# Order of two VectorE subtractions in the outputs' products of a hash-attention and feed-forward kernel

## The chip, the cores and the metric

The kernel runs on one core of a Trainium2 chip. The metric is the device time of one execution in microseconds, as a median over several runs. The engines of the core work side by side, each through its own queue: TensorE (PE in the profile) multiplies matrices, VectorE (DVE) and GpSimd (POOL) do elementwise work, ScalarE (ACT) does activations and copies, SyncE (SP) issues most of the transfers. [...]

## The reference

Attention in which a query sees the keys of its own hash bucket, and behind it a feed-forward block with a quick GELU. All numbers are 32-bit floats.

```
def _attn_setup():
    batch, n_heads, seq, head_dim = (4, 8, 768, 64)
...
    mask = q_bucket[:, :, :, None] == k_bucket[:, :, None, :]
    scores = scale * np.matmul(q, k.transpose(0, 1, 3, 2))
    scores = np.where(mask, scores, -1000000000.0)
...
    return np.matmul(attn, v).astype(np.float32)
...
def _moe_ref(x, w_in, w_out) -> np.ndarray:
    h = x @ w_in
    g = h * (1.0 / (1.0 + np.exp(-1.702 * h)))
    return (g @ w_out).astype(np.float32)
...
    x = np.ascontiguousarray(attn_out.transpose(0, 2, 1, 3)).reshape(B * S, H * D)
```

x is 3072 x 512, w_in 512 x 2048, g 3072 x 2048, w_out 2048 x 512. This case is about the last product, g @ w_out.

## The kernel before

The kernel has three stages: attention (to about 316 us of the span), the hidden layer x @ w_in with its GELU (to 594 us), and the outputs g @ w_out (from 594 us on). The order of the instructions of TensorE, VectorE, ScalarE and GpSimd is the order in which the program writes them; only SyncE's transfers are placed by the scheduler.

**Two levels of seven products.** The outputs are made in Strassen's manner (Winograd's variant, on two levels): instead of eight products of quarter matrices there are seven, of sums of the quarters. On the outer level the tokens come in 3 blocks of 1024, and each block takes the seven outer products in the order `OUTER` (L707). That makes 21 steps (`steps_out`, L1022). The outer sums of g were made and written to `g_dram` in the stage before. Each step is again done with seven inner products, `product_of_halves` (L1063).

**One step.** `fetch` (L1025) brings one outer operand of g (2 MB, in two halves of 1 MB) into one of two places that take turns: `raw_g` for even steps and a part of `s_in` for odd ones. Its four quarters are b11 and b12 (first half), b21 and b22 (second half); a quarter is 128 partitions x 4 x 256. Four subtractions, `sums_b` (L219 to L225), make the right operands of the inner products from them:

- t1 = b12 - b11 (L222)
- d12 = b22 - b12, written over b12 (L223)
- t2 = b22 - t1 (L224)
- t4 = b21 - t2 (L225)

t1, t2 and t4 have rooms of their own: t1a and t2a for even steps, t1b and t2b for odd ones (in step 1 a part of `t_x`), and one t4g. The left operands, quarters of w_out and their sums, are in SBUF; GpSimd makes the sums for later steps (`inner_sums`, L1232, behind a `mark`, L1231).

The products take their right operands in this order: product 1 b11, 2 b21, 3 b22, 6 t2, 7 d12, 5 t1, 4 t4 (`RIGHT`, L706, gives the place of each in the list b11, d12, b21, b22, t1, t2, t4; in the last step product 2 comes after product 5). A product is eight matmuls of 128x128 by 128x256 (L1074), each behind its own weight load. It goes to one of eight PSUM banks in turn. ScalarE copies products 1 and 3 out (L1087, L1090); VectorE adds the others up (L1078).

**Where the sums stand in VectorE's queue.** The sums of step n + 1 are issued during step n. `product_of_halves` calls `after(0)` to `after(3)` at four places between its additions, and `after` (L1237) picks from the list that `g_sums(n + 1)` (L1044) gives:

```
steps = [later_sums[at : at + 1]] if n == 0 else [[], later_sums[0:1], later_sums[1:3], later_sums[3:], []][at : at + 1]
```

So in a usual step the first of the list follows the additions of products 6 and 7, the second and third follow those of product 5, and the fourth follows that of product 4. In step 0 they go one to each place. In the last step but one `after(2)` gives the second and third in the same way, and the fourth stands between transposes. The sums of step 0 itself are issued at the end of the last two tiles of the hidden layer (L1216): `g_sums(0)[:1]` and `g_sums(0)[1:]`.

VectorE's queue also holds the outer additions (L1267, L1268) and the transposes of finished outputs into y (`turned`, L1049), which `written` (L1056) sends out.

Of the kernel before, what the change touches and what calls it, by code (L numbers as in the profile page):

```python
# [38 lines left out]
def kernel(  # L39
# [17 lines left out]
    nc = tc.nc  # L57
# [161 lines left out]
    def sums_b(eng, b11, b12, b21, b22, t1, t2, t4):  # L219


        return [lambda: eng.tensor_tensor(t1, b12, b11, op=Alu.subtract),  # L222
                lambda: eng.tensor_tensor(b12, b22, b12, op=Alu.subtract),  # L223
                lambda: eng.tensor_tensor(t2, b22, t1, op=Alu.subtract),  # L224
                lambda: eng.tensor_tensor(t4, b21, t2, op=Alu.subtract)]  # L225
# [472 lines left out]
    def feed_forward(tag, late=()):  # L698
# [9 lines left out]
        with ExitStack() as fctx:  # L708
# [313 lines left out]
            steps_out = [(sb, o) for sb in range(n1) for o in OUTER]  # L1022
# [10 lines left out]
            def g_quarters(n):  # L1033
                if n not in g_tiles:


                    g_tiles[n] = wholes[4:6] if n == 1 else [
                        (st2 if n % 2 else gp).tile([P, F4, TH], F32, tag=t, name=t + "ab"[n % 2]) for t in ("t1", "t2")]
                    g_tiles[n] = g_tiles[n] + [gp.tile([P, F4, TH], F32, tag="t4", name="t4g")]
                g = raw_g[n % 2]  # L1040
                x = [g[:, F4 * k : F4 * (k + 1), TH * j : TH * (j + 1)] for k in range(2) for j in range(2)]
                return x + g_tiles[n]

            def g_sums(n):  # L1044
                return sums_b(nc.vector, *g_quarters(n)) if n < len(steps_out) else [lambda: None] * 4

            ys = {}

# [152 lines left out]
            for n in range(2 * NESTED.stop, 3 * MT):  # L1201
                sb, mt = divmod(n, MT)
                if n == 2 * NESTED.stop + 1:
                    assert not agenda
                    inner_ctx.close()
                    twice_ctx.close()
                    cv_ctx.close()
                    sets[:] = [fctx.enter_context(tc.tile_pool(name=f"f{2 + i}{tag}", bufs=1, space=PSUM, side=side))
                               for i, side in enumerate(("right", "left"))]
                    gp = fctx.enter_context(tc.tile_pool(name=f"gp{tag}", bufs=1))  # L1210
                    raw_g[0] = gp.tile([P, FC // 2, XT], F32, name="raw_g")
                    t_ctx = fctx.enter_context(ExitStack())
                    places_of_sums.append(t_ctx.enter_context(tc.tile_pool(name=f"ts{tag}", bufs=1)))
                    outer_sums(*heads.pop("sums"))
                    fetch(0)
                t = {3 * MT - 2: g_sums(0)[:1], 3 * MT - 1: g_sums(0)[1:]}.get(n, []) if n > 3 * MT - 3 else []  # L1216
                hidden(sb, mt, between.get(n, []) + ([lambda: fetch(1)] if n == 3 * MT - 1 else []), t + todo.pop(n, []))
                yield
# [6 lines left out]
            for n, (sb, o) in enumerate(steps_out):  # L1225
# [6 lines left out]
                for f in {2: inner_sums(3), 3: inner_sums(4), 5: inner_sums(5) + inner_sums(6)[:2], 6: inner_sums(6)[2:]}.get(n, []):  # L1232
                    f()
                later_sums = g_sums(n + 1)
                m = wholes[n % len(wholes)]

# [91 lines left out]
```

## Time and profile before

| what | us |
|---|---|
| median of 3 runs (lowest, highest) | 859.61 (859.51, 860.23) |
| the profiled execution, its own time | 859.85 |
| its span | 858.0 |
| outputs' stage, 594 to 858: first product to last | 594.07 to 849.66 |
| one inner product, from start to start of the next | 1.73 |
| one subtraction of 128x1024 on VectorE, alone | 1.22 |
| the same beside GpSimd's sums (t2 of step 0, d12 of step 1) | 2.29, 2.28 |
| one addition of 128x256 on VectorE, alone | 0.42 |

Share of the engines in some stretches of the outputs' stage, each about one step (busy us; the last row is the tail):

| stretch, us | length | PE | DVE | POOL |
|---|---|---|---|---|
| 594.0 to 606.2 (step 0) | 12.20 | 12.20 | 11.79 | 10.34 |
| 606.2 to 618.3 (step 1) | 12.10 | 12.10 | 11.11 | 9.92 |
| 618.3 to 631.2 (step 2) | 12.90 | 12.26 | 12.52 | 5.73 |
| 631.2 to 644.0 (step 3) | 12.80 | 12.30 | 11.43 | 0.60 |
| 644.0 to 656.1 (step 4) | 12.10 | 12.10 | 8.32 | 7.14 |
| 837.4 to 858.0 (last step and tail) | 20.60 | 12.26 | 12.58 | 0.00 |

Times in the profile are microseconds from the span's start. A line of the order of time gives start, length, engine, line of the kernel, operation, out<-in, shape and count; in square brackets stands how long the engine was idle before it and what ended that, which is inferred from the events of the semaphores. PEld is TensorE's weight load. The ends of matmuls are modelled, so a product's cost is best read from the starts of two products.

### The profile page before, as it was taken

The numbers are of one execution on the slowest core, as the hardware profiler recorded it, in microseconds if no ns is written. First come the engines' busy times: TensorE is split into PE (matmuls) and PEld (weight loads), VectorE is DVE, ScalarE is ACT, GpSimd is POOL, SyncE is SP. The second block draws the span as 40 slices with busy tenths as digits, with TensorE's granted clock in tenths as the row PEclk, the third lists the DMA queues.
The fourth block names the chain that finished last, engine by engine and source line by source line (L and its number), as shares of the span: only waits on it lengthen the run. The fifth ranks groups of instructions, "written<-read, shape, count | busy, mean of one in ns | idle before, by whom it ended". The sixth has DMA issues, their size and how long they took to land.

```text
span 858.0 us, 13647 instructions
## 1 busy us (share of the span) xinstructions
PE 846.6 (99%) x5007; PEld 529.2 (62%) x5007; DVE 703.7 (82%) x1072; ACT 344.9 (40%) x549; POOL 353.4 (41%) x316
## 2 busy tenths in 40 slices
PE   9999999999999999999999999999999999999996
PEld 4444444444444444566666665545888888888885
DVE  4589999999999885788988788577998977797776
ACT  5866667777666644343443444433000000000000
POOL 4343333433333359996854476669724000000000
PEclk9999999999999999999999999999999999999998
DMA  5636655445653104435555646587744675467524
GB/s 130 98 52 107 105 94 85 85 86 100 116 91 75 47 26 152 142 143 226 199 201 213 221 162 231 196 292 252 264 165 166 198 258 194 155 191 245 196 99 101
DMA packets 160987, 132.11 MB, mean 154 GB/s; under 512 B 122608, under 2 KB 137616, under 8 KB 155536
## 3 DMA queue, kind: packets, MB, share of 16 engines
q1 hardware_dynamic: 152016, 106.63, 44.6%
q10 hardware_dynamic: 8896, 24.53, 8.3%
q8 instruction: 41, 0.67, 0.3%
q14 instruction: 34, 0.28, 0.1%
HBM read 79.69 MB, written 50.33 MB: 152 GB/s over the span
## 4 chain that ended last, share of the span: by engine, by line
PE 95%; DVE 3%; DMA 1%; issue 0%; ACT 0%; ACTq 0%; SPq 0%; DVEq 0%
PE product L1074 27%; PE product L751 22%; PE ps L435 18%; PE av L468 15%; PE small L819 6%; PE product L819 3%; PE dn L489 1%; DVE xT L1078 1%; PE hash L411 1%; DMA q<-in_q_dram 1%; DVE y L1054 1%; DVE v L1078 0%; PE hash L376 0%; DVE t2a L224 0%; DVE raw_g L223 0%
## 5 line engine op out<-in xcount | busy, mean ns | idle before, releaser
L436 ACT ACTIVATE e<-ps 128x768 f32<-128x768 f32 x192 | 151.2, 812 | 25.7 <-PE ps L435 23.1
L435 PE MATMUL ps<-qT,kT 64*128 64x384 f32 x768 | 155.1, 482 | 0.0
L443 POOL TENSOR_TENSOR acc<-e 128x768 f32<-128x768 f32 x32 | 51.8, 1618 | 194.0 <-ACT e L436 174.5
L468 PE MATMUL av<-e,v 128*32 128x385 f32 x1536 | 128.0, 487 | 0.0
L751 PE MATMUL product<-xT,w_in_sb 128*128 128x512 f32 x216 | 100.1, 593 | 0.1
L468 PEld LDWEIGHTS av<-e,v 128*32 128x32 f32 x1536 | 48.5, 109 | 76.2 <-issue 74.5
L435 PEld LDWEIGHTS ps<-qT,kT 64*128 64x128 f32 x768 | 68.0, 187 | 38.5 <-issue 38.4
L751 PE MATMUL product<-t_x,s_in 128*128 128x512 f32 x192 | 89.4, 592 | 0.0
L1087 ACT COPY u<-product 128x256 f32<-128x256 f32 x21 | 7.8, 372 | 173.4 <-PE product L1074 140.2
L751 PEld LDWEIGHTS product<-xT,w_in_sb 128*128 128x128 f32 x216 | 40.9, 190 | 36.5 <-issue 32.9
L435 PE MATMUL ps<-qf,kf 64*128 64x384 bf16 x384 | 62.9, 324 | 0.1
L444 POOL TENSOR_TENSOR acc<-acc,e 128x768 f32<-128x768 f32 x32 | 55.8, 1744 | 2.5
L751 PEld LDWEIGHTS product<-t_x,s_in 128*128 128x128 f32 x192 | 36.5, 190 | 29.7 <-issue 26.8
L449 DVE SCALAR_TENSOR_TENSOR acc<-e 128x768 f32<-128x768 f32 x32 | 47.7, 1490 | 5.1 <-ACT e L436 5.1
L767 DVE TENSOR_TENSOR u<-product,u 128x256 f32<-128x256 f32 (+1 forms) x60 | 28.4, 486 | 16.3 <-PE product L819 13.1
L435 PEld LDWEIGHTS <-kf 64*128 64x128 bf16 x384 | 18.9, 94 | 35.1 <-issue 6.2
L451 DVE TENSOR_TENSOR acc<-acc,e 128x768 f32<-128x768 f32 x32 | 34.3, 1072 | 3.3
L451 DVE TENSOR_TENSOR acc<-acc,acc 128x768 f32<-128x768 f32 x32 | 31.2, 974 | 6.3 <-POOL acc L444 3.2
L1074 PE MATMUL product<-raw_g,xT 128*128 128x256 f32 x152 | 35.1, 379 | 0.0
L222 POOL TENSOR_TENSOR u<-v,u 128x1024 f32<-128x1024 f32 (+1 forms) x11 | 23.8, 2165 | 22.1 <-ACT v L764 8.1
L767 DVE TENSOR_TENSOR v<-product,v 128x512 f32<-128x512 f32 x24 | 16.5, 689 | 19.4 <-PE product L751 19.4
L767 DVE TENSOR_TENSOR c<-small,c 128x256 f32<-128x256 f32 (+1 forms) x54 | 24.2, 461 | 8.8 <-PE small L819 8.6
(278 smaller groups left out, 1727.4 us busy)
## 6 DMA issues: line engine op xcount, KB each, us to landing
raw_g<-g_dram SPq DMA_DIRECT2D x22, 1024.0 KB
s_in<-g_dram SPq DMA_DIRECT2D x20, 1024.0 KB
g_dram<-c ACTq DMA_DIRECT2D x18, 512.0 KB
raw<-in_moe_w_out_dram ACTq DMA_DIRECT2D x16, 512.0 KB
raw<-in_moe_w_in_dram SPq DMA_DIRECT2D x15, 512.0 KB
v<-in_v_dram SPq DMA_DIRECT2D x32, 192.0 KB
k<-in_k_dram SPq DMA_DIRECT2D x60, 96.0 KB
q<-in_q_dram SPq DMA_DIRECT2D x60, 96.0 KB
```

The costliest lines, as they stand in the source:

```text
L222: return [lambda: eng.tensor_tensor(t1, b12, b11, op=Alu.subtract), lambda: eng.tensor_tensor(b12, b22, b12, op=Alu.subtract), lambda: eng ...
L435: nc.tensor.matmul(ps[:, j, 0:HS], a[hs, keys], m[hs, cols], start=not last, stop=last)
L436: nc.scalar.activation(es[c][:, kt, :, 0:HS], ps[:, :, 0:HS], Act.Exp, scale=1.0 / D**0.5)
L443: nc.gpsimd.tensor_tensor(acc, es[c][:, 0, :, 0:HS], es[c][:, 1, :, 0:HS], op=Alu.add)
L444: nc.gpsimd.tensor_tensor(acc, acc, es[c][:, 2, :, 0:HS], op=Alu.add)
L449: nc.vector.scalar_tensor_tensor(acc, e[0], T * TINY, e[1], op0=Alu.add, op1=Alu.add)
L451: nc.vector.tensor_tensor(acc, acc, x, op=Alu.add)
L468: nc.tensor.matmul(av[D * j + d : D * j + d + 32, :], vt[:, t, j, d : d + 32], es[c][:, t, j, :], start=(t == 0), stop=(t == T - 1))
L751: nc.tensor.matmul(ps, wq[LEFT[i]][:, kc, :], xq[RIGHT[i]][:, kc, :], start=(start and kc == 0), stop=(kc == K2 - 1), skip_group_check=not ...
L767: nc.vector.tensor_tensor(dst, x, y, op=Alu.add)
L819: nc.tensor.matmul(x, wq[LEFT[i]], xq[RIGHT[i]], start=start, stop=True, skip_group_check=True)
L1074: nc.tensor.matmul(ps, wq[LEFT[i]][:, c, :], gq[RIGHT[i]][:, c, :], start=(c == 0), stop=(c == F4 - 1))
```

## The change

`g_sums` gives the same four subtractions in another order: t1, t2, d12, t4. Since `after` and L1216 pick by position, t2 is issued where d12 was and d12 where t2 was, in all 21 steps. The other users of `sums_b` keep their order.

```
             def g_sums(n):
-                return sums_b(nc.vector, *g_quarters(n)) if n < len(steps_out) else [lambda: None] * 4
+                if n == len(steps_out):
+                    return [lambda: None] * 4
+                t1, d12, t2, t4 = sums_b(nc.vector, *g_quarters(n))
+                return [t1, t2, d12, t4]
```

In a usual step both stand next to each other in VectorE's queue. In step 0, which issues the sums of step 1, the additions of product 5 stand between them.

## The prediction

> **What bounds the kernel now.** I read the page's busy times and chain first, then TensorE's waits, then the order of time of three engines around the two waits found there. Steps are counted 0 to 20 as the kernel runs them (21 tiles of the outputs), and a step's seven products run in the order 1, 2, 3, 6, 7, 5, 4 (in the last 1, 3, 6, 7, 5, 2, 4).
>
> ```profile
> PE 846.6 (99%) x5007; PEld 529.2 (62%) x5007; DVE 703.7 (82%) x1072; ACT 344.9 (40%) x549; POOL 353.4 (41%) x316
> PE 95%; DVE 3%; DMA 1%; issue 0%; ACT 0%; ACTq 0%; SPq 0%; DVEq 0%
> ```
>
> TensorE is busy for 99% of the span and is 95% of the chain that ended last. So only time in which TensorE stands still can be won, and the outputs' stage has two such places (columns: total us, times, longest us; window from 560 us to the end):
>
> ```profile
> PE product L1074 <- DVE t2a L224: 0.6, 1, 0.6
> PE product L1074 <- ACT xT L1090: 0.5, 1, 0.5
> ```
>
> Matmuls in order of time (start, length, operands), products 3, 6, 7 of step 2 and then of step 3:
>
> ```profile
> 621.70 1.89 PE L1074 MATMUL product<-raw_g,w_in_sb 128*128 128x256 f32 x8
> 624.23 1.96 PE L1074 MATMUL product<-t2a,w_in_sb 128*128 128x256 f32 x8 [0.64 <-DVE t2a L224]
> 626.03 1.89 PE L1074 MATMUL product<-raw_g,xT 128*128 128x256 f32 x8
> ...
> 634.66 1.89 PE L1074 MATMUL product<-s_in,w_in_sb 128*128 128x256 f32 x8
> 637.05 1.96 PE L1074 MATMUL product<-t2b,w_in_sb 128*128 128x256 f32 x8 [0.49 <-ACT xT L1090]
> 638.85 1.89 PE L1074 MATMUL product<-s_in,w_out_sb 128*128 128x256 f32 x8
> ```
>
> Undisturbed, two products start 3.45 us apart (618.25 to 621.70), one 1.73. Here two take 626.03 - 621.70 = 4.33 and 638.85 - 634.66 = 4.19. The two places lose 0.88 and 0.74, together **1.62 us**; the waits' own 0.64 and 0.49 are less because a restarted product also runs 0.07 slower and matmul ends are modelled. No other product of the 21 steps starts late. Weight loads, where the wait sits:
>
> ```profile
> 621.49 1.70 PEld L1074 LDWEIGHTS product<-raw_g,w_in_sb 128*128 128x128 f32 x8
> 624.20 1.59 PEld L1074 LDWEIGHTS product<-t2a,w_in_sb 128*128 128x128 f32 x8 [1.01 <-ACT xT L1090]
> ...
> 634.45 1.70 PEld L1074 LDWEIGHTS product<-s_in,w_in_sb 128*128 128x128 f32 x8
> 637.01 1.59 PEld L1074 LDWEIGHTS product<-t2b,w_in_sb 128*128 128x128 f32 x8 [0.87 <-ACT xT L1090]
> ```
>
> And VectorE, which makes the operands:
>
> ```profile
> 621.73 1.21 DVE L223 TENSOR_TENSOR raw_g<-raw_g 128x1024 f32<-128x1024 f32 x1
> 622.87 1.21 DVE L224 TENSOR_TENSOR t2a<-raw_g,t1a 128x1024 f32<-128x1024 f32 x1
> ...
> 634.59 1.22 DVE L223 TENSOR_TENSOR s_in<-s_in 128x1024 f32<-128x1024 f32 x1
> 635.72 1.22 DVE L224 TENSOR_TENSOR t2b<-s_in,t1b 128x1024 f32<-128x1024 f32 x1
> ...
> 640.77 0.42 DVE L1078 TENSOR_TENSOR xT<-product,v 128x256 f32<-128x256 f32 x1 [1.24 <-PE product L1074]
> ```
>
> t2 ends at 622.87 + 1.21 = 624.08 and at 636.94; product 6, which reads it, loads its first weights at 624.20 and 637.01, 0.12 and 0.07 later. That the records name ScalarE's copy (c12, L1090) is a coincidence: the copy follows product 3's end by its own 0.4 us and happens to end at 636.96. In step 4 product 6 starts at 649.21, before that copy even starts (649.41). So **t2 is the last thing product 6 waits for, in steps 2 and 3 only**, and d12, made just ahead of it, is not read until product 7, one product later. VectorE is late there because of work before: from 614.99 to 640.77 its only idle time is 0.20 us, so it paces itself.
>
> **The change, part by part.** Nothing is added or removed; two subtractions of 128x1024 change places, in each of the 21 steps. Both wait for the half of g that holds b22 and t1 came before either, so no fetch is needed earlier; t2's room was last read by product 6 two steps before, over 20 us back; no DMA is issued by either. VectorE's total stays: 1.13 us from the start of the one to the start of the next, in either order.
>
> *Step 2.* t2 takes d12's place: 621.73 to 622.94. Product 6's weights are due at 621.49 + 1.73 = 623.22, later than 622.94 + 0.12 = 623.06: the wait is gone, with 0.16 to spare. TensorE is 0.88 ahead. d12 now ends at 624.08; product 7's weights are due at 623.22 + 1.73 = 624.95, so 0.87 is left.
>
> *Step 3.* VectorE has no wait that the 0.88 could shorten, so t2 comes in d12's place at 634.59 to 635.81, released at 635.88. Product 6's weights are due at 634.45 - 0.88 + 1.73 = 635.30: a wait of 0.58 **stays**. They start at 635.88 instead of 637.01, which is **1.13 us** earlier. So the two gains do not add to 1.62: the second place decides, and it moves by the one subtraction that was ahead of t2. d12 ends at 636.94, product 7's weights are due at 635.88 + 1.62 (637.01 to 638.63) = 637.50: 0.56 left. Behind that load TensorE's whole queue would wait.
>
> *From step 4 on.* VectorE's next wait, 1.24 before 640.77, is for product 7 of step 3; with that 1.13 earlier it shrinks to 0.11, and VectorE, its banks, POOL's marked sums and SyncE's refills (released by products and by t4) follow 1.13 earlier. What is late next: in steps 4 to 20 product 6 already finds t2 ready (least slack 0.22, step 6: 672.95 against weights at 673.17; it gains 1.13), and product 7 finds d12 ready with at least that slack plus 1.73, as d12 takes t2's old end. In steps 0 and 1 nothing waits before or after (d12 ends by about 598.3 and 610.8, product 7's weights at 600.76 and 612.85). In the tail (last step) VectorE's line runs through both subtractions whatever their order, after a wait for TensorE, so it moves as a block. If that cover failed, a slow d12 beside POOL (2.28 in step 1 against 1.22) would cost 2.28 - 1.22 - 0.56 = 0.5 in step 3; but POOL has no work from 631.8 to 648.7 there.
>
> *A new wait.* Before, product 7 needed no signal of its own for d12, since t2 came after it. Now it needs one, 21 times. The trace does not show that exact wait. Lower bound 0: product 6 waits for t2 by its own signal in every step, and where it is satisfied (the 19 steps other than 2 and 3) product 7 follows 1.72 to 1.73 later, like any other. Upper bound: the 0.14 from t2's end to the first matmul at a stall that really waits (624.09 to 624.23), times 21 = 2.9. I take 0, the same kind of wait on the same queue.
>
> [...]
>
> *Sum:* 859.85 (the profiled execution: span 858.0 and 1.85 around it) - 1.13 = 858.72; that execution lies 0.24 above the median of 859.61, so the median should be **858.5** (0.13% less).
>
> **Rivals.** A change under 0.2% (1.72 us) is about what a measurement of this kernel can't tell from none.
>
> 1. *Both places close*: 858.0. For it: both waits name nothing else. Against: VectorE has no gap between 626.8 and 636 to make t2 of step 3 earlier. It would need 0.58 us, for instance from the contended 1.24 to 1.94 us adds at 629.4 to 632.5 beside POOL. Even this is within 0.2%.
> 2. *Gain taken back later*: 859.6. A refill of g or a drain that is hidden by less than 1.13 in one of steps 4 to 20 catches TensorE up. Against: in the 200 us from 637 TensorE never waits, and refills are released by TensorE itself. For: their slack is not shown. That the order of the two instructions does not reach the chip gives the same time; VectorE's queue is kept in written order, so hardly possible.
> 3. *The new wait costs* (the slower side): product 7 pays for its own signal in every step. With c per step the time is 858.5 + 21c; from c = 0.054 it is slower at all, from (1.72 + 1.13)/21 = 0.136 slower by over 0.2%. At the bound, 0.14, 861.4. Against: product 6's satisfied waits.
> 4. *More than is lost now*: faster by over 1.72 would need TensorE time outside the two places, for instance VectorE beside POOL in another phase. All that TensorE loses in the steps is 1.62, so this needs the tail (about 8 us after the last matmul) to shrink too.
>
> **How the numbers follow.** Forecast 0.58, rival 1 0.12, rival 2 0.13, rival 3 0.10 (slower by over 0.2% in most of that), rival 4 0.07. Rival 1 and the forecast can pass 1.72 only with the runs' own spread (859.51 to 860.23, 0.7 us); I put 0.10 of their 0.70 there. So: faster 0.17, same 0.74, slower 0.09. The range runs from rival 1 less half that spread, 857.7, to rival 2 with a little of it, 859.8; it leaves out most of rival 3 and rival 4.
>
> **What would show it.** Right: t2 starts near 621.7 and 634.6 in the new trace, TensorE has no wait in step 2 and one of some 0.5 for t2 in step 3, VectorE's wait of 1.24 is nearly gone, the chain of the 200 us after starts 1.1 earlier and the tail is as long as before. Wrong: a wait of product 7 for d12 (L223), products farther apart than 1.73, a new wait for a transfer, or no wait at all in step 3 (rival 1). A time above 859.8 or below 857.7 would make the prediction wrong.

## The result and the profile after

The changed kernel takes 858.70 us (median of 22 runs, 857.98 to 859.58) against 859.75 (22 runs, 859.02 to 861.25): 1.05 us less, a ratio of 0.9987 with a 95% interval of 0.9982 to 0.9993. The interval leaves out 1, so it is faster, by 0.13%. Its profiled execution spans 856.8 us.

From the page of the changed kernel, busy times and the chain's shares by engine:

```profile
PE 846.2 (99%) x5007; PEld 529.2 (62%) x5007; DVE 703.3 (82%) x1072; ACT 344.9 (40%) x549; POOL 353.4 (41%) x316
PE 96%; DVE 2%; DMA 1%; ACT 0%; issue 0%; ACTq 0%; SPq 0%; DVEq 0%
```

The work is the same (703.3 us of VectorE against 703.7), and TensorE still makes up nearly all of the chain. TensorE's waits in the outputs' stage (total us, times, longest):

```profile
PE product L1077 <- issue: 0.2, 1, 0.2
```

Two waits of 0.6 and 0.5 us have become one of 0.2, for which the record names no other engine ("issue"). Products 3, 6 and 7 of step 2, then of step 3, in order of time (a matmul line moved from L1074 to L1077):

```profile
621.45 1.89 PE L1077 MATMUL product<-raw_g,w_in_sb 128*128 128x256 f32 x8
623.17 1.89 PE L1077 MATMUL product<-t2a,w_in_sb 128*128 128x256 f32 x8
624.90 1.89 PE L1077 MATMUL product<-raw_g,xT 128*128 128x256 f32 x8
...
633.53 1.89 PE L1077 MATMUL product<-s_in,w_in_sb 128*128 128x256 f32 x8
635.67 1.97 PE L1077 MATMUL product<-t2b,w_in_sb 128*128 128x256 f32 x8 [0.25 <-issue]
637.47 1.89 PE L1077 MATMUL product<-s_in,w_out_sb 128*128 128x256 f32 x8
```

The weight load of product 6 of step 3:

```profile
635.64 1.59 PEld L1077 LDWEIGHTS product<-t2b,w_in_sb 128*128 128x128 f32 x8 [0.62 <-issue]
```

From product 3 to product 7, step 2 now takes 624.90 - 621.45 = 3.45 us, undisturbed, and step 3 takes 3.94, so 0.49 is still lost there. The gain is 4.33 - 3.45 = 0.88 in step 2 and 4.19 - 3.94 = 0.25 in step 3, 1.13 in all. VectorE in the same stretch:

```profile
621.49 1.21 DVE L224 TENSOR_TENSOR t2a<-raw_g,t1a 128x1024 f32<-128x1024 f32 x1
622.62 1.21 DVE L223 TENSOR_TENSOR raw_g<-raw_g 128x1024 f32<-128x1024 f32 x1
...
634.35 1.22 DVE L224 TENSOR_TENSOR t2b<-s_in,t1b 128x1024 f32<-128x1024 f32 x1
635.49 1.22 DVE L223 TENSOR_TENSOR s_in<-s_in 128x1024 f32<-128x1024 f32 x1
...
639.40 0.42 DVE L1081 TENSOR_TENSOR xT<-product,v 128x256 f32<-128x256 f32 x1
```

The two subtractions have changed places and nothing else moved against them. VectorE's wait of 1.24 for product 7 of step 3 has shrunk to 0.10 (the addition before it ends at 639.30), where 0.11 was forecast; the same addition of step 2, whose product is long done, starts 0.11 behind as well (628.60, then 628.71), so hardly a wait is left. t2 of step 3 ends at 634.35 + 1.22 = 635.57; product 6 loads its first weights 0.07 later and starts 0.10 later, so t2 is still what it waits for. ScalarE's copy of product 3 can't be: it ends at 635.46 + 0.37 = 635.83, behind product 6's start.

**A better measure than the span.** The starts in the two profiles differ by 0.25 us before the outputs begin (593.82 and 594.07). The distance from the first to the last product of the stage leaves that out: 847.77 - 594.07 = 253.70 before, 846.40 - 593.82 = 252.58 after, 1.12 less. The experiments are compared by it. It leaves out what follows the last product's start, which matters for the last of them.

### The profile page after: what moved, and what is told of

It is laid out like the page before. It is cut to its first block, busy times and chain, and to the rows that moved or that the text cites. A ratio compares the mean times of both kernels' runs of the same rounds, so it can differ in the third digit from the quotient of the medians.

```text
span 856.8 us, 13648 instructions
## 1 busy us (share of the span) xinstructions
PE 846.2 (99%) x5007; PEld 529.2 (62%) x5007; DVE 703.3 (82%) x1072; ACT 344.9 (40%) x549; POOL 353.4 (41%) x316
## 4 chain that ended last, share of the span: by engine, by line
PE 96%; DVE 2%; DMA 1%; ACT 0%; issue 0%; ACTq 0%; SPq 0%; DVEq 0%
PE product L1077 28%; PE product L751 22%; PE ps L435 18%; PE av L468 15%; PE small L819 6%; PE product L819 3%; PE dn L489 1%; PE hash L411 1%; DVE xT L1081 1%; DVE y L1057 1%; DMA pj<-in_proj_dram 1%; PE hash L376 0%; DVE v L1081 0%; DVE raw_g L223 0%; DVE t2a L224 0%
## 5 line engine op out<-in xcount | busy, mean ns | idle before, releaser
L1077 PE MATMUL product<-raw_g,xT 128*128 128x256 f32 x152 | 35.1, 379 | 0.0
```

What stands on the lines that cost most here:

```text
L1077: nc.tensor.matmul(ps, wq[LEFT[i]][:, c, :], gq[RIGHT[i]][:, c, :], start=(c == 0), stop=(c == F4 - 1))
```

## The experiments

All stage lengths are from the first product's start to the last product's start of one profiled execution; an undisturbed step takes 3.45 from product 3 to product 7. The medians are set against runs of the kernel before that were taken beside each kernel.

| kernel | step 2, 3 to 7 | step 3, 3 to 7 | stage | against before |
|---|---|---|---|---|
| before | 4.33 | 4.19 | 253.70 | |
| changed | 3.45 | 3.94 | 252.58 | -1.12 |
| changed, once more | 3.46 | 3.94 | 252.57 | -1.13 |
| step 2 alone | 3.45 | 5.07 | 253.71 | +0.01 |
| step 3 alone | 4.31 | 3.45 | 252.96 | -0.74 |
| all but 2 and 3 | 4.33 | 4.19 | 253.69 | -0.01 |
| d12 last | 3.89 | 4.11 | 253.39 | -0.31 |
| no sums at step 2 | 3.45 | 3.46 | 252.09 | -1.61 |
| t2 behind t1 | 3.45 | 3.50 | 252.19 | -1.51 |
| three together | 3.46 | 3.51 | 252.14 | -1.56 |

### Do the two gains add up? Step 2 alone

```
-                return [t1, t2, d12, t4]
+                return [t1, t2, d12, t4] if n == 2 else [t1, d12, t2, t4]
```

> t2 ahead of d12 in step 2 alone, the old order in the other 20. My theory: step 2 loses its wait (product 3 to product 7: 4.33 us before, 3.45 now), TensorE reaches step 3 0.88 us earlier and stands there 0.88 longer, because VectorE's t2 of step 3 ends when it always did (product 3 to product 7 of step 3: 4.19 + 0.88 = 5.07). No gain at the end: the time of before within 0.2 us. Rival, each wait pays for itself: 0.88 us faster, step 3 unchanged at 4.19.

Measured: 859.58 us against 859.80 (ratio 0.9998, 0.9989 to 1.0007). Order of time of the matmuls in step 3 (the view ends inside product 7, so it shows three of its eight matmuls):

```profile
633.43 1.89 PE L1077 MATMUL product<-s_in,w_in_sb 128*128 128x256 f32 x8
636.70 1.97 PE L1077 MATMUL product<-t2b,w_in_sb 128*128 128x256 f32 x8 [1.38 <-ACT xT L1093]
638.50 0.81 PE L1077 MATMUL product<-s_in,w_out_sb 128*128 128x256 f32 x3
```

The wait removed in step 2 reappears in step 3: 0.49 has become 1.38, and 3.45 + 5.07 equals 4.33 + 4.19. **A wait taken away ahead of a later wait for the same late engine gains nothing by itself** here, where VectorE has no wait between the two. The rival, that each wait pays for itself, falls.

### Step 3 alone

```
-                return [t1, t2, d12, t4]
+                return [t1, t2, d12, t4] if n == 3 else [t1, d12, t2, t4]
```

> t2 ahead of d12 in step 3 alone. My theory: step 2 keeps its 4.33; in step 3 t2 ends 1.13 earlier, which is before TensorE, held up in step 2, asks for it, so step 3 takes 3.45 and the gain is 0.74 us. Rival, the gain of step 3 is what the changed kernel shows there (4.19 to 3.94): 0.25 us faster.

Measured: 858.92 against 859.80 (ratio 0.9992, 0.9983 to 1.0001), the stage 0.74 shorter. The interval reaches 1, so the gain is shown by the stage and not by the medians. In the order of time (the view ends inside the last product):

```profile
624.02 1.97 PE L1077 MATMUL product<-t2a,w_in_sb 128*128 128x256 f32 x8 [0.62 <-DVE t2a L224]
...
634.46 1.89 PE L1077 MATMUL product<-s_in,w_in_sb 128*128 128x256 f32 x8
636.18 1.89 PE L1077 MATMUL product<-t2b,w_in_sb 128*128 128x256 f32 x8
637.91 1.46 PE L1077 MATMUL product<-s_in,w_out_sb 128*128 128x256 f32 x6
```

Step 2 keeps its wait, and step 3's is wholly gone, since a TensorE that was held up in step 2 asks later. So 0.00 for one, 0.74 for the other, 1.12 for both: no split of the gain between the steps makes sense of all three, and the end of t2 in step 3, where VectorE's own pace puts it, makes sense of each.

### What does the new wait of product 7 cost? All steps but 2 and 3

```
-                return [t1, t2, d12, t4]
+                return [t1, d12, t2, t4] if n in (2, 3) else [t1, t2, d12, t4]
```

> t2 ahead of d12 in 19 steps, the old order in steps 2 and 3: 19 products 7 with a signal of their own and no wait removed. My theory: such a satisfied wait costs nothing, so steps 2 and 3 show 4.33 and 4.19 as before, products elsewhere start 1.72 to 1.73 apart, and the time is that of before within 0.2 us. Rival, the new wait costs c: 19 c slower, 1.0 us at 0.05 and 2.7 us at 0.14.

Measured: 859.76 against 859.80 (ratio 0.9998, 0.9989 to 1.0007), the stage 253.69 against 253.70. In the trace's semaphore records product 7's first weight load waits for VectorE in 18 of the 19 steps (not in the last), and in no step of the kernel before, so the waits are there. Together they change the stage by 0.01 us, no more than it differs between two executions of one kernel. Rival 3 of the prediction falls: at 0.054 us each, the least price that makes the kernel slower at all, they would have cost 1.0.

### How late may d12 be? d12 behind t4 for steps 2 and 3

```
-                return [t1, t2, d12, t4]
+                return [t1, t2, t4, d12] if n in (2, 3) else [t1, t2, d12, t4]
...
-                    steps = [later_sums[at : at + 1]] if n == 0 else [[], later_sums[0:1], later_sums[1:3], later_sums[3:], []][at : at + 1]
+                    steps = [later_sums[at : at + 1]] if n == 0 else [[], later_sums[0:1], later_sums[1 : 2 if n in (1, 2) else 3], later_sums[2 if n in (1, 2) else 3 :], []][at : at + 1]
```

> For steps 2 and 3 d12 comes last, behind t4, which puts off its end by 0.34 + 1.13 = 1.47 us; t2 as in the changed kernel. It tests the margins given for product 7 (0.87 and 0.56 us of lateness allowed). My theory: product 7 now waits, in step 2 by 1.47 - 0.87 = 0.6, in step 3 until d12 ends: product 3 to product 7 about 4.1 in step 2; step 3's product 7 starts about where it did before the change, 0.1 to 0.2 earlier, so nearly all of the 1.13 us is given back. Rival, product 7 does not read d12 so soon or the margin is larger: 3.45 and 3.94 as in the changed kernel.

One execution, 859.05 us, read by its stage. Matmuls in order of time, products 6, 7 and 5 of step 2 and product 7 of step 3:

```profile
622.84 1.89 PE L1077 MATMUL product<-t2a,w_in_sb 128*128 128x256 f32 x8
625.00 1.99 PE L1077 MATMUL product<-raw_g,xT 128*128 128x256 f32 x8 [0.27 <-DVE raw_g L223]
626.83 1.89 PE L1077 MATMUL product<-t1a,w_in_sb 128*128 128x256 f32 x8
...
637.85 1.99 PE L1077 MATMUL product<-s_in,w_out_sb 128*128 128x256 f32 x8 [0.49 <-DVE s_in L223]
```

Product 7 does wait for d12 (L223) in both steps, so the margin was real and of about the size given: product 6 is in time, and product 7 has become the place that decides. The sizes were off. Step 2 shows 3.89 where I expected about 4.1, and of the 1.12 the kernel keeps 0.31 where I expected 0.1 to 0.2. The margin was worked out on weight loads, and by them it holds: product 7's load was due at 624.36 and came at 625.00, 0.64 late. But an undisturbed first matmul starts 0.21 behind its load (622.63 and 622.84), and after a stall it starts with it (both at 625.00), so product 7 itself is only 625.00 - 624.57 = 0.43 late, and then runs slower by 0.10 (1.83 to product 5), 0.53 lost in all.

### Why is VectorE late there? GpSimd without its sums at step 2

```
-                for f in {2: inner_sums(3), 3: inner_sums(4), 5: inner_sums(5) + inner_sums(6)[:2], 6: inner_sums(6)[2:]}.get(n, []):
+                for f in {3: inner_sums(4), 5: inner_sums(5) + inner_sums(6)[:2], 6: inner_sums(6)[2:]}.get(n, []):
```

> The order of before, and GpSimd leaves out the four sums of w_out that stand at step 2 (613.98 to 619.40 us, operands of step 3), so the output is not the reference's from step 3 on. My theory: those sums are why VectorE is late: its additions beside them take 1.41 and 2.90 (two) in place of 0.42 and 0.88. Without them VectorE is 3.0 us earlier, t2 is in time in both steps, both take 3.45, and the kernel gains the whole 1.62 us without the change. Rival, VectorE is late by its own amount of work: the additions stay as slow, and 4.33 and 4.19 stay.

The order of the subtractions is that of before. In the kernel before, three of VectorE's additions beside GpSimd's sums took 1.41 and 2.90:

```profile
615.31 1.26 POOL L215 TENSOR_TENSOR w_out_sb<-w_out_sb 128x512 f32<-128x512 f32 x1
615.45 1.41 DVE L1078 TENSOR_TENSOR v<-v,xT 128x256 f32<-128x256 f32 x1
...
616.53 1.45 POOL L216 TENSOR_TENSOR w_in_sb<-w_in_sb,w_out_sb 128x512 f32<-128x512 f32 x1
616.78 2.90 DVE L1078 TENSOR_TENSOR xT<-xT 128x256 f32<-128x256 f32 x2
```

Without the sums, in one execution (859.32 us, with a stage that begins 0.90 later than in the profile of before), the same additions and then t2:

```profile
616.35 0.42 DVE L1078 TENSOR_TENSOR v<-v,xT 128x256 f32<-128x256 f32 x1
616.70 0.88 DVE L1078 TENSOR_TENSOR xT<-xT 128x256 f32<-128x256 f32 x2
...
620.76 1.22 DVE L224 TENSOR_TENSOR t2a<-raw_g,t1a 128x1024 f32<-128x1024 f32 x1
```

t2 of step 2 starts 1.84 us ahead of product 3 (622.60) where it started 1.17 behind it before: 3.0 earlier. No product of the stage waits, and the stage is 1.61 shorter, with the old order. So without three additions slowed beside GpSimd's sums, some 6 us ahead of the first wait and 20 ahead of the second, neither wait arises. For the second wait they are not the whole cause: in the kernel before the additions of step 3 (at 629.43 and 630.59) took 1.24 and 1.94 beside GpSimd's next sums, 1.9 us more than alone. In this run they took 1.53 and 0.87, because GpSimd's sums of step 3 ran earlier too: they end at 628.43 + 1.26 = 629.69, before the second of these starts (629.90). No run leaves out those sums alone. What the runs show is the pair of times, 1.41 beside GpSimd's sums and 0.42 without them; why an addition takes longer beside them is not shown.

### A version that gains more? t2 directly behind t1

```
-                    steps = [later_sums[at : at + 1]] if n == 0 else [[], later_sums[0:1], later_sums[1:3], later_sums[3:], []][at : at + 1]
+                    steps = [later_sums[at : at + 1]] if n == 0 else [[], later_sums[0:2], later_sums[2:3], later_sums[3:], []][at : at + 1]
```

It ran beside the changed kernel once more, on the same chip.

> The changed kernel once more, beside the next three on one chip. Product 3 to product 7 takes 3.45 us in step 2 and 3.94 in step 3; 1.1 us faster than before.

> In a usual step t2 comes directly behind t1, ahead of the two additions of product 5 (0.67 us from start to start), d12 where it is in the changed kernel. My theory: what the changed kernel still loses in step 3, 0.49 us, is t2's lateness behind VectorE's own queue; with t2 0.67 earlier (less some 0.1 that an operation right behind the one it reads may wait) it is ready when product 6 asks, so steps 2 and 3 both take 3.45 to 3.5 and the time is 1.5 to 1.62 us under before, 0.4 to 0.5 under the changed kernel. Rival, the rest of the wait belongs to ScalarE's copy of product 3, as the records of before name it: step 3 stays at 3.94.

Measured: the changed kernel 859.11 (ratio 0.9990, 0.9981 to 0.9999), t2 behind t1 859.03 (0.9988, 0.9979 to 0.9998). By their medians the two can't be told apart, so the 0.4 to 0.5 us expected between them do not show there. By the stage they can: 252.57 and 252.19. Step 3 in order of time:

```profile
633.79 1.89 PE L1077 MATMUL product<-s_in,w_in_sb 128*128 128x256 f32 x8
635.52 1.93 PE L1077 MATMUL product<-t2b,w_in_sb 128*128 128x256 f32 x8
637.29 1.94 PE L1077 MATMUL product<-s_in,w_out_sb 128*128 128x256 f32 x8
639.07 1.89 PE L1077 MATMUL product<-t1b,w_in_sb 128*128 128x256 f32 x8
```

Product 6 starts at its due time, 1.73 behind product 3. That the records of before name ScalarE's copy of product 3 as the releaser was indeed a coincidence: here the copy can't have ended when product 6 starts at 635.52, as product 3 itself ends at 633.79 + 1.89 = 635.68. What is left is small: products 6 and 7 each take 1.77 to 1.78 to the next, since t2 and now d12 hold back their first weight loads, by 0.15 and 0.16 (the second at 637.24, due 1.62 behind the stalled load at 635.46).

### All three together

```
-                    steps = [later_sums[at : at + 1]] if n == 0 else [[], later_sums[0:1], later_sums[1:3], later_sums[3:], []][at : at + 1]
+                    steps = [later_sums[at : at + 1]] if n == 0 else [[], later_sums[0:3], [], later_sums[3:], []][at : at + 1]
```

> In a usual step t1, t2 and d12 come together behind the additions of products 6 and 7, both additions of product 5 after them. With t2 behind t1 but d12 behind the additions, step 3 still lost 0.05 at product 6 and 0.05 at product 7, which had come to wait for d12. My theory: d12 now ends 0.67 us earlier and product 7 no longer waits; product 6 is as late as there, by the restart of a weight load (0.05). Product 3 to product 5 of step 3: 5.23 us (5.28 with d12 behind the additions, 5.18 undisturbed). First to last product of the stage: 252.1 to 252.15 us (253.70 before, 252.58 changed), so 1.55 to 1.6 us under before. Rival: the additions of product 5, put off by 1.13 us more, hold back a PSUM bank, c12 or what follows, and TensorE waits at another place of the 21 steps: over 252.2.

Measured: 858.62 against 859.93 (ratio 0.9986, 0.9977 to 0.9995). The stage is 252.14; product 3 to product 5 of step 3 takes 638.31 - 633.08 = 5.23. Product 7 no longer waits, and no other place does. To the last product this is the shortest stage that leaves nothing out, 0.44 below the changed kernel's.

That the whole kernel gains as much is not shown. Its interval overlaps the changed kernel's, and part of the 0.44 is lost again further on. From 834.14 us on the chain that ended last in the kernel before runs through VectorE and ScalarE, no longer through TensorE. VectorE's last transpose ends 849.02 + 0.63 - 593.37 = 256.28 us after the stage's first product, against 849.75 + 0.63 - 593.82 = 256.56 in the changed kernel: 0.28 less, not 0.44. Of the 0.16 between, 0.12 are seen in the sums for the last step, which lie on that chain: t2 follows t1 by 835.08 - 833.83 = 1.25 there, where two subtractions that don't depend on each other follow by 1.13. To the end of the span 0.1 to 0.2 is left (856.2 - 593.37 = 262.83 against 856.8 - 593.82 = 262.98); where the rest goes is not shown.

## Why the prediction was right

- **The sum.** Forecast 1.13 us; 1.13 in the two steps and 1.12 over the stage; 1.05 between the medians (858.70 against a forecast of 858.5, where 0.14 of the difference is that before itself came out at 859.75 in 22 runs and at 859.61 in the 3 shown). The two steps and the stage bear out the mechanism; that the medians agree to 0.1 is in part luck, as single runs of one kernel spread by 1.6 to 2.2 us.
- **Step 2**: forecast no wait and 0.88, measured 3.45 and 0.88.
- **Step 3**: forecast that a wait stays because VectorE paces itself. It stays, with 0.49 lost. On the weight load it was forecast at 0.58 and is 635.64 - (633.32 + 1.73) = 0.59. The prediction lets VectorE pace itself until 640.77; the stretch without a wait ends at 639.54, where the 1.24 begin, which changes nothing in step 3. The load was forecast 1.13 earlier than before; against the stage's first product it is 637.01 - 594.07 = 42.94 before and 635.64 - 593.82 = 41.82 after, 1.12. That the gains don't add was the step most open to doubt, and the two kernels with one step changed show it directly.
- **Product 7's slack**: forecast 0.87 and 0.56 from d12's end to the weight load, measured 624.68 - 623.83 = 0.85 and 637.26 - 636.71 = 0.55.
- **Step 4 on**: no wait, the products 1.73 apart, as forecast. Rival 2 (taken back later) falls: the gain at step 3 is the gain at the last product, and VectorE's last transpose still ends 1.14 earlier (256.56 us after the stage's first product, 257.70 before).
- **The new wait at 0**: shown. In the kernel with all steps but 2 and 3 changed, 18 such waits go with a stage of 253.69 us, against 253.70 without them. The prediction counts 21 such waits; the records show one on product 7 in 20 steps, all but the last.
- **Rival 1** (both places close) falls for this change, as step 3 still waits; the later kernels reach it, to within some 0.1 us, only by making t2 of step 3 earlier by another 0.44 to 0.45 (it starts 40.53 us after the stage's first product in the changed kernel, 40.08 and 40.09 in those two) or by taking GpSimd's sums away.
- **Rival 4** (more than is lost now, out of the tail) falls: from the last product's start to the end of the span it is 858.0 - 847.77 = 10.2 us before and 856.8 - 846.40 = 10.4 after. The span's 1.2 us are 0.25 from ahead of the stage and 1.12 in it, less some 0.2 of the tail and of rounding. Why the tail varies stays open: what follows VectorE's last transpose takes 6.2 to 6.6 us in the ten profiled executions.
- **What only the margins got wrong**: lateness counted on weight loads overstates by about 0.2 how late the first matmul is, and by about 0.1 what is lost once the slower product behind it is counted (0.64 against 0.43 and 0.53 in the kernel with d12 last). They also leave out the 0.05 to 0.12 us from an operand's end to the load that it releases. The forecast escaped it, because it compared the same event, a stalled load, before and after.

## What to carry to other kernels

Order operands in the producer's queue by when the consumer asks for them, but first find the *last* wait of the consumer for that producer: here nothing was won unless its release moved, and no more than it moved (1.13 us forecast, the work that was ahead; 1.12 measured). Waits removed before it just gather there: alone they won 0.00 here, and together with it they brought 0.74 up to 1.12. When the producer hardly idles between two such waits, its own pace, not the consumer's, sets the second: in the kernel before VectorE was idle for 0.20 us between 614.99 and 639.54, and with step 2 alone changed the 0.88 won there was lost again in step 3. And look further back for why the producer is late: here three additions beside another engine's work cost 3 us, more than the reordering could hide. Last, follow the chain to the end of the program: time won on one engine counts in full only if the engines that end the program don't lose it again (with all three together, 0.44 us at the last product became 0.28 at VectorE's last transpose).

## What the runs showed that was not expected

- **Runs of one kernel spread by more than this change, and the spread has a place.** The 22 runs of before lie between 859.02 and 861.25. In the ten profiled executions the stage's first product starts between 593.37 and 594.97 us. Most of that is there from the first hash matmul on, which starts between 8.07 and 9.38, behind transposes of the first inputs; in five of the ten the records show these waiting 0.28 to 0.92 us for the transfer of q. The way from it to the outputs' stage is 585.2 to 585.8 in all ten. The stage's length of one kernel repeats to 0.01 (252.58 and 252.57).
- **A stalled weight load costs less than it shows and a little more later.** Its first matmul starts almost with it (0.00 to 0.06) and not 0.21 behind; the product then runs 1.77 to 1.83 in place of 1.73.
- **An operation right behind the one it reads starts later.** In the kernel with t2 behind t1, t2 starts 0.03 after t1's end (619.94 + 1.21, then 621.18), where an unrelated addition starts 0.07 before it (619.93 + 1.21, then 621.07, in the kernel before). In the last step, where that line is on the chain, it is part of what three together lost again.
